# Row sums of one pair of heads taken from ScalarE and given to GpSimd and VectorE, in a fused attention and mixer kernel

## The chip, the core and the metric

The kernel runs on one core of a Trainium2 chip. The metric is the device time of one execution in microseconds, lower being better. PE is TensorE, DVE is VectorE, ACT is ScalarE, POOL is GpSimd, SP is the queue that issues the DMAs.

## What is computed

Four batches of eight heads go through a banded attention, and its result goes through a two-step mixer. Cut to what matters here:

```python
scores_l = scale * q @ k.T                       # kept where |row - column| < 16
scores_s = scale * q @ k_sum.T + log(32)         # k_sum: maxima of 32 keys each
a = exp(scores_all - rowmax(scores_all))
a = a / (sum(a, axis=-1, keepdims=True) + 1e-9)  # the row sums of this change
x = a @ concat([v, v_sum])                       # v_sum: means of 32 values each
h = relu(x.T @ w_tok1) @ w_tok2;  u = x + h.T    # token mixer
out = u + relu(u @ w_ch1) @ w_ch2                # channel mixer
```

## The kernel before

Each batch has four pairs of heads, and each pair's 768 rows are worked off as six tiles of 128 rows, in two groups g of three. For a pair p and a group g, `scores` lets PE make two tiles of products `sc` (one for each head of the pair, 128 x 360). DVE then handles one tile row at a time in `lowest` (L527): it scales, adds the mask, writes the result to `e` and leaves the row's minimum of the negated scores in `den[:, 1]`. ACT follows in `power` (L537): it takes the exponential in place and leaves the row sum in `den[:, 0]`, by its accumulator, which costs a second instruction (ACTIVATION_READ_ACCUMULATOR) behind each exponential. There are 12 exponentials per pair. PE turns `e` around (`et`, L575), ACT copies the turned tile out (`eT`, L586), and PE multiplies it with the values (`av`, L645). POOL adds 1e-9 to the six row sums (`rec`, L651), DVE takes the reciprocal (L671) and scales the product into `x` (L656).

Beside that run, for the first batch: DVE's maxima of the next pair's keys (`ks`, L381) and their copy into the key tile (L390), which the next pair's `sc` needs; the value means, summed by PE (`vm`, L407), copied by ACT (L418), joined by DVE (L428, L421) and POOL (L433); and the unpacking of the mixer's weights, in steps ("ticks") of 512 KB. A tick passes from ACT (L1711) to POOL (L1715), to three steps of DVE (L1720, L1727, L1734), and, for all but the first three, on to ACT (L1758) and POOL (L1764), which split a weight into a high and a low part. The first three ticks make `wt1`, the operand of the first mixer product `t1p` (L799); ticks 3 to 5 make `wt2h` and `wt2l`, those of `up` (L966); later ones, with tiles named `wb_6`, `wb_7`, `wb_8`, ..., make the channel mixer's, of which `hp` (L1027) is the first product. A tick's tile `wb` has two buffers at this place, so tick 8 waits until POOL has read tick 6's.

The order on each engine is not written by hand. Every piece of work is given to `Plan.add` with a rank and a guessed duration; the planner walks through a model of the machine and writes each engine's instructions in the order that comes out. `PLACES` overrides the place of single pieces, which it names by their number in the order of the `add` calls. Each engine then works strictly in its order.

Of the kernel before, what the change touches and what calls it, by code (L numbers as in the profile page):

```python
# [14 lines left out]
AF = mybir.ActivationFunctionType  # L15
ALU = mybir.AluOpType
AX = mybir.AxisListType.X
# [6 lines left out]
P = 128  # L24
# [4 lines left out]
NC = WIN + NB  # L29
NP = H // 2  # L30
VB = NP * NB
TT = S // P
# [39 lines left out]
class Work:  # L72
# [5 lines left out]


PLACES = {  # L80
# [11 lines left out]
}  # L92


# [151 lines left out]
def tile_attention_mixer(  # L246
# [13 lines left out]
    nc = tc.nc  # L260
# [6 lines left out]
    add = plan.add  # L267

    def sbuf(shape, tag, name, bufs, dtype=F32):
        return plan.slot(sb, shape, dtype, tag, name, bufs)  # L270
# [10 lines left out]
        out=means[:, NB - 2 : NB],  # L281
        in_=identf[:WIN, 16 : 16 + QT].rearrange("p (r c) -> p r c", c=32),
        axis=AX, op=ALU.add,
# [203 lines left out]
    def scores(p, g, behind=()):  # L487

        kt, qt = k_t[p], q_t[p]
        tiles = []  # L490
        e = e_t[p, g] = sbuf([P, 2, HS], "e", f"e_{p}_{g}", 3)
        if p >= FAR * NP:

            add(
                "pool", 0.2,
                lambda: nc.gpsimd.memset(
                    e.t.rearrange("p j (t c) -> p (j t) c", c=P)[:, :, NC:], 0.0
                ),
                writes=[(e, "ends")], rank=R_LATER,
            )  # L500
        for j in range(2):
            n = 2 * p + j
            if g == 0:
                den_t[n] = sbuf([P, 2, TT], "den", f"den_{n}", 5)
            tiles.append(att_bank(f"sc_{n}_{g}"))

        def products():
            for i in range(TT // 2):
                for c in range(2):
                    t = 2 * (TT // 2 * g + i) + c  # L510
                    for j in range(2):
                        rows = slice(j * D, (j + 1) * D)
                        nc.tensor.matmul(  # L513
                            tiles[j].t[c * QT : (c + 1) * QT, i * NC : (i + 1) * NC],
                            lhsT=qt.t[rows, t * QT : (t + 1) * QT], rhs=kt.t[rows, t, :],
                            start=True, stop=True,
                        )

        add(
            "pe", 0.95, products, reads=[(qt, 0), (kt, 0), (kt, 1)],  # L520
            writes=[(t, 0) for t in tiles], rank=R_H, behind=behind,
        )

        def lowest(n, j, i):
            T = TT // 2 * g + i
            mv = 0 if T == 0 else (2 if T == TT - 1 else 1)
            nc.vector.tensor_tensor_reduce(  # L527
                out=e.t[:, j, i * P : i * P + NC],
                in0=tiles[j].t[:, i * NC : (i + 1) * NC],
                in1=mask_sb[:, mv, :], op0=ALU.add, op1=ALU.min,  # L530
                scale=-1.0 / 8.0, scalar=3.0e38, accum_out=den_t[n].t[:, 1, T : T + 1],
            )

        def power(n, j, i):
            T = TT // 2 * g + i
            ei = e.t[:, j, i * P : i * P + NC]
            nc.scalar.activation(  # L537
                ei, ei, AF.Exp, bias=den_t[n].t[:, 1, T : T + 1], scale=-1.0,
                accum_out=den_t[n].t[:, 0, T : T + 1],
            )  # L540

        for i in range(TT // 2):
            for j in range(2):
                n = 2 * p + j
                den, T = den_t[n], TT // 2 * g + i
                add(
                    "dve", 0.21, lambda n=n, j=j, i=i: lowest(n, j, i), reads=[(tiles[j], 0), ("mask", 0)],
                    writes=[(e, (j, i)), (den, ("min", T))], rank=R_ATT,
                )
                add(  # L550
                    "act", 0.39, lambda n=n, j=j, i=i: power(n, j, i), reads=[(den, ("min", T))],
                    writes=[(e, (j, i)), (den, ("sum", T))], rank=R_ATT,
                )


    FAR = 2
# [1386 lines left out]
```

## Time and profile before

| | us |
|---|---|
| median of 3 runs | 556.57 (556.07, 556.57, 558.44) |
| the profiled execution | 557.6 |
| its span, from the first to the last instruction | 555.8 |
| PE busy in the span | 543.1 |
| ACT busy, DVE busy, POOL busy | 251.8, 330.6, 246.7 |

The span is what the views of the trace divide up; 1.8 us of the profiled execution's time lie outside it. A busy PE is one with a product under way. [...]

### The profile page before, as it was taken

To read this page: it belongs to the slowest core of one execution; us is meant where nothing else is said; L and a number is where in the kernel's file an instruction comes from. 1 tells how busy PE (TensorE), PEld (TensorE's weight loads), DVE (VectorE), ACT (ScalarE), POOL (GpSimd) and SP (SyncE) were. 2 spreads that over 40 slices of the span, in tenths; PEclk is the share of its full clock that TensorE was granted. 3 is DMA by queue.
4 is the path that set the end of the run, shared out by engine and by line. 5 is a ranking of instruction groups with operands and counts; after the bars stand their busy time and mean duration, and the time that the engine had idled before them with its cause. 6 is when DMAs were issued, how large, how long until landed. Compare 5 with 4: busy or idle time off the path is not lost.

```text
span 555.8 us, 12577 instructions
## 1 busy us (share of the span) xinstructions
PE 543.1 (98%) x4549; PEld 478.7 (86%) x4549; DVE 330.6 (59%) x922; ACT 251.8 (45%) x784; POOL 246.7 (44%) x362
## 2 busy tenths in 40 slices
PE   7799999999999999999999999999999999999997
PEld 4589788889989878888799987878889999999997
DVE  5897799988463355553553257344352066569992
ACT  5895666526485443322414325243433443356410
POOL 0356688726383933310058404467869853000000
PEclk9999999999999999999999999999999999999999
DMA  8992568745658147867676216787696543932732
GB/s 294 343 255 85 184 197 261 245 131 190 228 163 256 38 153 208 224 190 210 160 229 157 96 30 202 164 235 199 168 276 147 135 166 116 317 102 86 238 113 86
DMA packets 125743, 101.10 MB, mean 182 GB/s; under 512 B 70000, under 2 KB 105456, under 8 KB 125680
## 3 DMA queue, kind: packets, MB, share of 16 engines
q1 hardware_dynamic: 125680, 100.29, 60.8%
q8 instruction: 36, 0.59, 0.5%
q14 instruction: 27, 0.22, 0.1%
HBM read 70.18 MB, written 28.31 MB: 177 GB/s over the span
## 4 chain that ended last, share of the span: by engine, by line
PE 88%; DVE 5%; POOL 3%; ACT 2%; issue 1%; POOLq 0%; DVEq 0%; ACTq 0%
PE acc L1070 28%; PE hp L1027 27%; PE sc L513 4%; PE av L645 4%; PE t1q L883 3%; PE up L966 3%; PE x L1297 2%; PE y L1297 2%; PE z L1297 2%; PE pz L1297 2%; PE up L1259 2%; PE pw L1297 1%; PE pv L1297 1%; PE px L1297 1%; PE pr L1297 1%; PE w L1297 1%
## 5 line engine op out<-in xcount | busy, mean ns | idle before, releaser
L1070 PE MATMUL acc<-h,w2h 128*128 128x256 f32 (+1 forms) x576 | 153.9, 339 | 0.0
L1027 PE MATMUL hp<-u,w1h 128*128 128x256 f32 (+1 forms) x576 | 143.9, 339 | 0.3 <-DVE u L1010 0.3
L1070 PEld LDWEIGHTS acc<-h,w2h 128*128 128x128 f32 x576 | 100.5, 188 | 13.9 <-ACT h L1039 1.7
L1027 PEld LDWEIGHTS hp<-u,w1h 128*128 128x128 f32 x576 | 98.0, 189 | 12.9 <-issue 1.1
L1027 PE MATMUL hp<-u,w1l 128*128 128x256 f32 (+1 forms) x288 | 96.9, 336 | 0.0
L1070 PE MATMUL acc<-h,w2l 128*128 128x256 f32 (+1 forms) x288 | 96.4, 335 | 0.0
L537 ACT ACTIVATE e<-e,den 128x120 f32<-128x120 f32 x192 | 73.5, 385 | 48.8 <-DVE den L527 37.9
L1044 DVE SCALAR_TENSOR_TENSOR h<-hp,h 128x512 fp32r<-128x512 f32 (+1 forms) x72 | 39.8, 552 | 83.9 <-ACT h L1039 83.8
L1039 ACT ACTIVATE h<-hp 128x512 fp32r<-128x512 f32 (+1 forms) x72 | 35.1, 487 | 104.2 <-PE hp L1027 104.0
L1027 PEld LDWEIGHTS hp<-u,w1l 128*128 128x128 f32 x288 | 54.4, 189 | 5.8
L1070 PEld LDWEIGHTS acc<-h,w2l 128*128 128x128 f32 x288 | 54.2, 188 | 5.2
L527 DVE CUSTOM_DVE_ANT_0 e<-sc,mask_sb 128x120 f32<-128x120 f32 x192 | 41.8, 277 | 14.9 <-PE sc L513 14.3
L537 ACT ACTIVATION_READ_ACCUMULATOR e<-e,den 128x1 f32 x192 | 36.3, 189 | 0.0
L651 POOL TENSOR_SCALAR rec<-den 128x6 f32<-128x6 f32 x32 | 8.5, 266 | 58.7 <-ACT e L537 57.0
L1110 POOL TENSOR_TENSOR ot<-ot,u 128x512 f32<-128x512 f32 (+1 forms) x24 | 24.4, 1045 | 21.4 <-DVE ot L1102 19.9
L469 DVE TENSOR_REDUCE vs<-vb 96x8 f32<-96x256 f32 (+1 forms) x40 | 18.0, 461 | 21.0 <-DMA vb<-in_vb 20.7
L513 PE MATMUL sc<-k,q 64*64 64x120 f32 x768 | 27.7, 271 | 2.2 <-DVE k L390 1.2
L513 PEld LDWEIGHTS sc<-k,q 64*64 64x64 f32 x768 | 20.3, 132 | 10.8 <-issue 7.9
L645 PEld LDWEIGHTS av<-v,eT 120*64 120x64 f32 x768 | 24.1, 138 | 5.3 <-issue 3.5
L966 PE MATMUL up<-wt2h,t 128*128 128x512 f32 (+1 forms) x96 | 28.4, 353 | 0.1
L645 PE MATMUL av<-v,eT 120*64 120x64 f32 x768 | 26.7, 224 | 1.3 <-DVE den L527 0.8
L381 DVE TENSOR_REDUCE ks<-k 128x24 f32<-128x768 f32 x16 | 15.1, 946 | 19.9 <-DMA k<-in_kw 19.8
(248 smaller groups left out, 1042.5 us busy)
## 6 DMA issues: line engine op xcount, KB each, us to landing
w<-in_w_ch SPq DMA_DIRECT2D x48, 256.0 KB
k<-in_kw SPq DMA_DIRECT2D x16, 720.0 KB
v<-in_vw SPq DMA_DIRECT2D x32, 288.0 KB
q<-in_q SPq DMA_DIRECT2D x16, 384.0 KB
away<-e SPq DMA_DIRECT2D x16, 384.0 KB
eT<-away SPq DMA_DIRECT2D x64, 96.0 KB
w<-in_w_tok SPq DMA_DIRECT2D x12, 256.0 KB
vb<-in_vb SPq DMA_DIRECT2D x32, 96.0 KB
```

The costliest lines, as they stand in the source:

```text
L469: lambda: nc.vector.tensor_reduce(out=s.t[:VB, rows], in_=slot.t[:VB], axis=AX, op=ALU.add),
L513: nc.tensor.matmul(tiles[j].t[c * QT : (c + 1) * QT, i * NC : (i + 1) * NC], lhsT=qt.t[rows, t * QT : (t + 1) * QT], rhs=kt.t[rows, t, :], ...
L527: nc.vector.tensor_tensor_reduce(out=e.t[:, j, i * P : i * P + NC], in0=tiles[j].t[:, i * NC : (i + 1) * NC], in1=mask_sb[:, mv, :], op0=A ...
L537: nc.scalar.activation(ei, ei, AF.Exp, bias=den_t[n].t[:, 1, T : T + 1], scale=-1.0, accum_out=den_t[n].t[:, 0, T : T + 1],)
L645: nc.tensor.matmul(pv[cs, T], lhsT=eT[:NC, T % (TT // 2), cs], rhs=v.t[:NC, 2 * T + c], start=True, stop=True,)
L966: nc.tensor.matmul(pt.t[:, :nt], lhsT=t1.t[:, part, ks], rhs=w.t[:, k, h0 : h0 + nt], start=(far and k == 0 and i == 0), stop=(k == DTOK / ...
L1027: nc.tensor.matmul(pt.t[:, :nt], lhsT=block(w, f, c), rhs=us[c].t[:, part], start=(i == 0), stop=(i == len(ops) - 1),)
L1039: lambda: nc.scalar.activation(h.t[:, 0], pt.t[:, :nt], AF.Relu),
L1044: lambda: nc.vector.scalar_tensor_tensor(out=h.t[:, 1], in0=pt.t[:, :nt], scalar=0.0, in1=h.t[:, 0].bitcast(F32), op0=ALU.max, op1=ALU.sub ...
L1070: nc.tensor.matmul(slot.t[:, c0 : c0 + nt], lhsT=block(w, f, o), rhs=h.t[:, part], start=(f == 0 and w == "w2h" and part == 0 and o % n == 0),
L1110: lambda view=view, u=u: nc.gpsimd.tensor_tensor(out=view(), in0=view(), in1=u.t[:, 1].bitcast(F32), op=ALU.add),
L1297: nc.tensor.matmul(pt.t[:, :cols], lhsT=w[wp][0](), rhs=z.t[:, zp], start=first and seen == 0, stop=final and seen == 3 * len(ops) - 1, sk ...
```

## The change

For the first pair alone (p = 0), the exponentials of ACT no longer use the accumulator. The row sums come from a new function, `totals`, called once for each group: POOL adds three strips of 40 columns of `e` onto each other for all six tile rows (two additions of 128 x 240), folds the 40 columns to 20 (one addition of 128 x 120), and DVE sums the 20 columns, in one reduction for each of the two heads (128 x 3 results). That is 6 additions and 4 reductions for the pair. The tile `some` of the partial sums has one buffer, shared with a tile that the start of the program uses for warming up PE. All other pairs keep the accumulator. Ten more pieces of work stand in the list, so later pieces have other numbers, and `PLACES` holds another set of places altogether; two of its lines stand here for all.

```diff
 PLACES = {
-    6: (0, 3.73), 23: (1, 279.8), 30: (1, 279.88), 34: (1, 88.42), 36: (1, 279.87),
+    4: (0, 3.2), 6: (0, 2.9), 16: (2, 32.7), 35: (2, 13.2), 36: (2, 126.1), 39: (2, 13.7),
...
             ei = e.t[:, j, i * P : i * P + NC]
+            total = den_t[n].t[:, 0, T : T + 1] if p >= 1 else None
             nc.scalar.activation(
-                ei, ei, AF.Exp, bias=den_t[n].t[:, 1, T : T + 1], scale=-1.0,
-                accum_out=den_t[n].t[:, 0, T : T + 1],
+                ei, ei, AF.Exp, bias=den_t[n].t[:, 1, T : T + 1], scale=-1.0, accum_out=total
             )
...
+        if p < 1:
+            totals(p, g)
+
+    def totals(p, g):
+        e, third = e_t[p, g], NC // 3
+        some = sbuf([P, TT, third], "vb", f"some_{p}_{g}", 1)
+        def part(i):
+            return e.t.rearrange("p j (t c) -> p (j t) c", c=P)[:, :, i * third : (i + 1) * third]
+        def more(a, b):
+            nc.gpsimd.tensor_tensor(out=some.t, in0=a(), in1=b(), op=ALU.add)
+        def fold():
+            nc.gpsimd.tensor_tensor(
+                out=some.t[:, :, : third // 2], in0=some.t[:, :, : third // 2],
+                in1=some.t[:, :, third // 2 :], op=ALU.add,
+            )
...
+        for j in range(2):
...
+                lambda j=j, den=den, T=T: nc.vector.tensor_reduce(
+                    out=den.t[:, 0, T : T + TT // 2],
+                    in_=some.t[:, TT // 2 * j : TT // 2 * (j + 1), : third // 2],
+                    axis=AX, op=ALU.add,
+                ),
```

What the change moves was read from the order of the instructions before and after. On all engines the order differs up to about the first ten products of the channel mixer's first sums and is the same from there to the end. In names such as `sc_2_0` the first number is the head, the second the group.

On ACT, the twelve exponentials of the first pair stand group by group (before, the two groups are mixed), and three copies of turned tiles (`eT`) stand among them instead of one. On PE, the turns of the first pair that follow `et_0_0`, namely `et_1_0` and `et_0_1`, come before `sc_2_0`, not after it. On SP, the loads of `q_3` and `k_3` stand ahead of `v_4`, not behind it; `v_7` stands behind the two halves of tick 5; the other loads up to the channel weights keep their places.

DVE, from the key maxima of pair 1 on. Before:

```order
L381 TENSOR_REDUCE ks_1_170<-k_1_99 128x24
L527 ISA e_0_1_156,den_0_141<-sc_0_1_126,mask_sb_71 128x120
L527 ISA den_0_141 128x1
L390 COPY k_1_99<-ks_1_170 128x12x24
L527 ISA e_0_1_156,den_1_143<-sc_1_1_127,mask_sb_71 128x120
L527 ISA den_1_143 128x1
L671 RECIPROCAL rec_0_201<-rec_0_201 128x6
L527 ISA e_1_0_231,den_2_232<-sc_2_0_186,mask_sb_71 128x120
```

After:

```order
L392 COPY k_1_99<-ks_1_180 128x12x24
L529 ISA e_0_1_162,den_1_149<-sc_1_1_127,mask_sb_71 128x120
L529 ISA den_1_149 128x1
L591 TENSOR_REDUCE den_0_141<-some_0_0_177 128x3
L591 TENSOR_REDUCE den_1_149<-some_0_0_177 128x3
L529 ISA e_1_0_228,den_2_229<-sc_2_0_205,mask_sb_71 128x120
...
L591 TENSOR_REDUCE den_0_141<-some_0_1_222 128x3
L591 TENSOR_REDUCE den_1_149<-some_0_1_222 128x3
L430 TENSOR_TENSOR vs_0_0_282<-vm_0_231,vs_0_0_282 24x64
L423 TENSOR_TENSOR v_1_103<-vm_0_231,vs_0_0_282 24x768
L716 RECIPROCAL rec_0_289<-rec_0_289 128x6
```

The reductions stand where DVE has finished a group's scores, so DVE comes to them in its order whether POOL's additions are done or not.

PE, between the products of the third pair and the first mixer product. Before:

```order
L575 MATMUL et_4_0_499<-identf_66,e_2_0_423 120x128 x3
L575 MATMUL et_5_0_520<-identf_66,e_2_0_423 120x128 x3
L575 MATMUL et_4_1_529<-identf_66,e_2_1_495 120x128 x3
L407 MATMUL vm_2_534<-v_4_330,means_72 24x64
...
L575 MATMUL et_5_1_588<-identf_66,e_2_1_495 120x128 x3
L799 MATMUL t1p_0_0_597<-x_0_0_357,wt1_371 128x128 x12
```

After:

```order
L620 MATMUL et_4_0_514<-identf_66,e_2_0_403 120x128 x3
L620 MATMUL et_5_0_533<-identf_66,e_2_0_403 120x128 x3
L409 MATMUL vm_2_542<-v_4_375,means_72 24x64
...
L620 MATMUL et_4_1_596<-identf_66,e_2_1_510 120x128 x3
L620 MATMUL et_5_1_602<-identf_66,e_2_1_510 120x128 x3
L844 MATMUL t1p_0_0_608<-x_0_0_373,wt1_406 128x128 x12
```

One turn, `et_4_1`, has gone behind `vm_2` and `sc_6_0`; otherwise the same work stands ahead of `t1p_0_0`.

DVE, where the last `x` of the batch are made and ticks 6 to 8 pass (`t1p_0_3` on PE needs both). Before:

```order
L785 SCALAR_TENSOR_TENSOR t1_0_2_830<-t1p_0_2_793,t1_0_2_830 128x256
L656 TENSOR_TENSOR x_0_1_694<-av_6_817,rec_6_765 128x6x64
L1720 TENSOR_SCALAR wb_6_815<-wb_6_815 128x512
L656 TENSOR_TENSOR x_0_1_694<-av_7_833,rec_7_772 128x6x64
L1727 SCALAR_TENSOR_TENSOR wb_6_815<-w_6_514,wb_6_815 128x512
L1720 TENSOR_SCALAR wb_7_848<-wb_7_848 128x512
L1734 SCALAR_TENSOR_TENSOR wb_6_815<-w_6_514,wb_6_815 128x512
```

After:

```order
L430 TENSOR_TENSOR vs_0_3_822<-vm_3_786,vs_0_3_822 24x64
L423 TENSOR_TENSOR v_7_519<-vm_3_786,vs_0_3_822 24x768
L1779 SCALAR_TENSOR_TENSOR wb_6_769<-w_6_524,wb_6_769 128x512
L1765 TENSOR_SCALAR wb_7_847<-wb_7_847 128x512
L1772 SCALAR_TENSOR_TENSOR wb_7_847<-w_7_708,wb_7_847 128x512
L1055 TENSOR_TENSOR u_0_0_0_873<-up_0_0_0_831,u_0_0_0_873 128x512
L701 TENSOR_TENSOR x_0_1_675<-av_7_855,rec_7_773 128x6x64
L1779 SCALAR_TENSOR_TENSOR wb_7_847<-w_7_708,wb_7_847 128x512
L1765 TENSOR_SCALAR wb_8_896<-wb_8_896 128x512
L701 TENSOR_TENSOR x_0_1_675<-av_6_902,rec_6_771 128x6x64
```

The `x` of head 6 has gone behind the first DVE step of tick 8 (L1765, before L1720), and tick 6's last DVE step ahead of both `x`.

## Rows read from the trace of the kernel before

**Rows 1.** Busy time of each engine in three stretches of the span: length, then busy us and instructions of PE, of PE's weight loads, of DVE, ACT and POOL, granted clock, DMA share, GB/s.

```profile
8.30:30.00 21.70, 15.30 (x356) 11.59 (x360) 18.70 (x94) 19.95 (x88) 5.39 (x10) 1.00 1.04 325
30.00:61.00 31.00, 30.53 (x404) 27.49 (x392) 26.48 (x72) 22.22 (x69) 19.45 (x26) 1.00 0.55 163
61.00:555.80 494.80, 490.16 (x3744) 436.62 (x3744) 282.94 (x750) 208.13 (x627) 221.11 (x319) 1.00 0.60 175
```

**Rows 2.** Who waited for whom in the first 90 us, PE alone: us in total, times, longest.

```profile
PE et L575 <- DVE x L656: 1.4, 2, 1.1
PE sc L513 <- DVE k L390: 1.2, 1, 1.2
...
PE et L575 <- ACT eT L586: 1.0, 2, 0.6
```

**Rows 3.** Timeline of PE: start, us, then the instructions merged, with the idle time before them and what ended it. The first `sc` is `sc_2_0`, the second `sc_6_0`; the `vm` is `vm_2`; the three `t1p` are `t1p_0_0`, `t1p_0_2` and `t1p_0_3`.

```profile
11.22 1.08 PE L513 MATMUL sc<-k,q 64*64 64x120 f32 x24 [1.18 <-DVE k L390]
...
29.52 0.87 PE L407 MATMUL vm<-v,means 96*24 96x64 f32 x48
30.32 0.84 PE L513 MATMUL sc<-k,q 64*64 64x120 f32 x24
31.09 0.54 PE L575 MATMUL et<-identf,e 128*120 128x128 f32 x3
31.48 2.84 PE L799 MATMUL t1p<-x,wt 128*128 128x128 f32 x24
...
41.86 2.84 PE L799 MATMUL t1p<-x,wt 128*128 128x128 f32 x24
...
51.77 2.84 PE L799 MATMUL t1p<-x,wt 128*128 128x128 f32 x24
...
60.94 0.73 PE L1027 MATMUL hp<-u,w1h 128*128 128x512 f32 x2 [0.32 <-DVE u L1010]
```

**Rows 4.** Timeline of ACT, in the same columns: the first exponential of the program and the next, the turned copy among them, two copies that follow each other, and the last exponential of the first pair.

```profile
8.05 0.39 ACT L537 ACTIVATE e<-e,den 128x120 f32<-128x120 f32 x1 [6.05 <-DVE den L527]
8.35 0.18 ACT L537 ACTIVATION_READ_ACCUMULATOR e<-e,den 128x1 f32 x1
8.44 0.38 ACT L537 ACTIVATE e<-e,den 128x120 f32<-128x120 f32 x1
...
10.71 0.47 ACT L586 ACTIVATE eT<-et 120x384 f32<-120x384 f32 x1
11.08 0.38 ACT L537 ACTIVATE e<-e,den 128x120 f32<-128x120 f32 x1
...
12.97 0.38 ACT L537 ACTIVATE e<-e,den 128x120 f32<-128x120 f32 x1
...
13.46 0.44 ACT L418 ACTIVATE vs<-vm 24x64 f32<-24x64 f32 x2
...
44.66 0.72 ACT L1758 ACTIVATE wt2h<-wb 128x256 fp32r<-128x256 f32 x2 [1.47 <-DVE wb L1734]
```

**Rows 5.** Timeline of DVE: the copy of pair 1's keys, the end of the last scores of the first pair, the first scores of the second, a wait for its other group, the copy of pair 3's keys and the last two steps of `wt1`.

```profile
10.82 0.31 DVE L390 COPY k<-ks 128x288 f32<-128x288 f32 x1
...
11.24 0.08 DVE L527 DVE_READ_ACCUMULATOR2_ANT den<- 128x1 f32 x1
...
12.34 0.28 DVE L527 CUSTOM_DVE_ANT_0 e<-sc,mask_sb 128x120 f32<-128x120 f32 x1 [0.23 <-PE sc L513]
...
18.88 0.28 DVE L527 CUSTOM_DVE_ANT_0 e<-sc,mask_sb 128x120 f32<-128x120 f32 x1 [0.88 <-PE sc L513]
...
29.77 0.30 DVE L390 COPY k<-ks 128x288 f32<-128x288 f32 x1
29.99 0.68 DVE L1727 SCALAR_TENSOR_TENSOR wt<-w,wt 128x512 int32<-128x512 int32 x1
...
30.71 0.69 DVE L1734 SCALAR_TENSOR_TENSOR wt<-w,wt 128x512 int32<-128x512 int32 x1
31.32 0.28 DVE L527 CUSTOM_DVE_ANT_0 e<-sc,mask_sb 128x120 f32<-128x120 f32 x1
```

**Rows 6.** POOL's subtractions of 128 x 256 in its timeline, two by two: the first two beside DVE's L527, the second two beside DVE's weight steps; and, from the page, its additions of 128 x 512 (us of all, then mean ns of one).

```profile
36.78 1.43 POOL L1764 TENSOR_TENSOR wt2l<-wb,wt2h 128x256 fp32r<-128x256 f32 x2
...
50.17 2.52 POOL L1764 TENSOR_TENSOR w1l<-wb,w1h 128x256 fp32r<-128x256 f32 x2 [2.06 <-ACT w1h L1758]
L1110 POOL TENSOR_TENSOR ot<-ot,u 128x512 f32<-128x512 f32 (+1 forms) x24 | 24.4, 1045 | 21.4 <-DVE ot L1102 19.9
```

**Rows 7.** The one DVE reduction of few elements in the program (busy us, mean ns).

```profile
L280 DVE TENSOR_REDUCE means<-identf 96x2 f32<-96x64 f32 x1 | 0.2, 216 | 0.2 <-POOL identf masks.py:199 0.2
```

**Rows 8.** Ticks 6 and 8 in the timelines of DVE, ACT and POOL: the DVE step behind `t1p_0_2` and the `x` after it; tick 6's last DVE step; tick 8's ACT step, POOL step and first DVE step, with the idle time before each.

```profile
46.26 0.43 DVE L785 SCALAR_TENSOR_TENSOR t<-t1p,t 128x256 fp32r<-128x256 f32 x1 [1.64 <-ACT t L780]
46.60 0.55 DVE L656 TENSOR_TENSOR x<-av,rec 128x384 f32<-128x384 f32 x1
...
48.96 0.68 DVE L1734 SCALAR_TENSOR_TENSOR wb<-w,wb 128x512 int32<-128x512 int32 x1
...
52.73 0.76 ACT L1711 ACTIVATE wb<-w 128x256 f32<-128x256 f32 x2 [1.78 <-POOL w1l L1764]
53.65 0.61 POOL L1715 TENSOR_SCALAR wb<-wb 128x512 f32<-128x512 f32 x1 [0.95 <-ACT wb L1711]
54.30 0.95 DVE L1720 TENSOR_SCALAR wb<-wb 128x512 int32<-128x512 int32 x1 [2.19 <-POOL wb L1715]
```

**Rows 9.** Busy share of the DMA engines from 5 to 28.5 us, in 40 slices, in tenths.

```profile
DMA  9999899999999999999999999999999999999999
```

More of the change, by code (lines that the diff above doesn't have):

```diff
@@ L550, in scores @@
                 add(
-                    "act", 0.39, lambda n=n, j=j, i=i: power(n, j, i), reads=[(den, ("min", T))],
-                    writes=[(e, (j, i)), (den, ("sum", T))], rank=R_ATT,
-                )
+                    "act", 0.39 if p >= 1 else 0.22, lambda n=n, j=j, i=i: power(n, j, i),
+                    reads=[(den, ("min", T))],
+                    writes=[(e, (j, i))] + [(den, ("sum", T))] * (p >= 1), rank=R_ATT,
+                )
+        if p < 1:
[12 more added lines that the diff above has]
+            )
+        parts = [(e, (j, i)) for j in range(2) for i in range(TT // 2)]
+        add(
+            "pool", 0.7, lambda: more(lambda: part(0), lambda: part(1)), reads=parts,
+            writes=[(some, 0)], rank=R_ATT,
+        )
+        add(
+            "pool", 0.7, lambda: more(lambda: some.t, lambda: part(2)), reads=parts,
+            writes=[(some, 0)], rank=R_ATT,
+        )
+        add("pool", 0.45, fold, writes=[(some, 0)], rank=R_ATT)
+        for j in range(2):
+            den, T = den_t[2 * p + j], TT // 2 * g
+            add(
+                "dve", 0.14,
+                lambda j=j, den=den, T=T: nc.vector.tensor_reduce(
[3 more added lines that the diff above has]
+                ),
+                reads=[(some, 0)],
+                writes=[(den, ("sum", T + i)) for i in range(TT // 2)], rank=R_ATT,
+            )
     FAR = 2
```

22 rows, old and new, of the table PLACES are left out of this document.

## The prediction

> **What bounds the kernel now.** The first view to read is busy time by stretch [rows 1]. From 61 us to the end PE is busy for 490.2 of 494.8 us, and from 30 to 61 us for 30.5 of 31.0. Only from 8.3 to 30 us, while the first attention batch gets going, does PE have slack: 15.30 of 21.70 us busy, 6.40 us idle. Since the change leaves the order alone behind the channel mixer's first products, all it can give back is these 6.40 us and the 0.47 us of the next stretch. It removes no PE work.
>
> The second view, who waited for whom on PE, says what that slack is [rows 2]: many short waits, mostly for DVE (its `x`, its key copy) and for ACT's turned copies. The third look is at the two engines that feed PE there: ACT is busy for 19.95 of 21.70 us and DVE for 18.70 [rows 1]. So DVE has only 3.00 us of idle time to give up, and DVE is what ends the slack: the key copy of pair 3 is done at 29.99 and `sc_6_0`, which needs it, starts at 30.32; the last step of `wt1` is done at 31.32 and `t1p_0_0` starts at 31.48 [rows 3, 5]. From there on PE has enough to do.
>
> **ACT's part.** Before, an exponential and its read-out step ACT by 0.39 us (8.05 to 8.44), and the last of the first pair's twelve ends at 12.97 + 0.38 = 13.35 [rows 4]. Without the read-out no such exponential is in the trace. Two copies of 64 columns take 0.44 us together and two of 256 columns 0.72, so 120 columns lie between 0.22 and 0.36 each; I take 0.25, nearer the smaller. A turned copy steps ACT by 0.37 (10.71 to 11.08) [rows 4]. Three of them now stand among the twelve: 8.05 + 12 x 0.25 + 3 x 0.37 = 12.16, so the pair is 1.2 us earlier with two more copies behind it. The first group is done at 8.05 + 6 x 0.25 = 9.55.
>
> **POOL's part.** Its additions have no row of their own. The subtractions of 256 columns beside DVE's L527 took 1.43 us for two, 0.715 each; the additions of 512 columns 1.045 on average [rows 6]. That is 1.3 ns a column: 0.695 for 240 columns, 0.54 for 120, so a chain of 0.695 + 0.695 + 0.54 = 1.93 us for each group. The upper bound is the pair that took 2.52 us, 1.26 each [rows 6], which would make a chain 3.4 us; it ran beside DVE's weight steps, of which there are none here yet, so I stay at the lower row. The chains end at 9.6 + 1.93 = 11.55 and 12.2 + 1.93 = 14.15. POOL has 16 us of idle time in this stretch [rows 1], which hides the 3.9 us; the two `rec` and the `v` copy queued behind the chains are due only when DVE has made `v_1`, a us later.
>
> **DVE's part.** Four reductions are added. The bounds are 0.10 each and the 0.216 of the one small reduction [rows 7]; with 20 columns in six rows I take 0.14, 0.56 in all. They also make DVE wait in its own order, with pair 1's scores queued behind the first two and the `v_1` step behind the last two. It comes to the first at about 11.25 (the last read-out of the first pair is at 11.24 [rows 5]) and waits 0.3 us for POOL. `sc_2_0` now stands behind `et_0_1`, whose third exponential is done at 9.55 + 0.37 + 4 x 0.25 = 10.92; with a turn of 0.39 (31.09 to 31.48 [rows 3]) it starts near 11.4, not 11.22. Its scores begin 1.12 us after it, as before (11.22 to 12.34 [rows 3, 5]), near 12.5: a wait of 0.65 after the reductions. Six scores end at 13.75, and the second chain's sums come at 14.15: 0.4 more. Together 1.35, say 1.4 with the handovers. In return the old waits go: the second group of pair 1, for which DVE sat idle 0.88 us until 18.88 [rows 5], is on PE some 4 us sooner (11.4 + 0.77 + a turn of 0.39 + a `vm` of 0.80, then 1.1 to its scores: 14.5), and DVE has work in hand from 14.5 on. The same steps stand ahead of `wt1`'s last one in both orders, so it ends at 31.32 - 3.00 + 1.4 + 0.56 = 30.3, 1.0 us earlier. The key copy of pair 3 now stands behind one more weight step of 0.60: 29.99 - 1.04 + 0.60 = 29.55.
>
> **PE's part.** `sc_6_0` starts at 29.6 rather than 30.32, 0.7 us sooner, but one turn that stood ahead of it now follows (0.39). With 0.77 for `sc_6_0` (30.32 to 31.09) and two turns, `t1p_0_0` starts at 29.6 + 0.77 + 0.78 = 31.15, not 31.48 [rows 3]: **0.3 us gained**. Half a dozen waits in front of it disappear into this one figure, since DVE is last either way.
>
> From there two more places count. `t1p_0_3`, at 51.77 before, could start at 51.45, but the `x` that it needs now stands on DVE behind tick 8's first step, which came at 54.30, released by POOL [rows 8]. Tick 8 is earlier too. Four items that preceded `t1p_0_2` on PE now follow it (a `vm` of 0.80 and three turns, 1.17), so it starts at 41.86 - 0.3 - 2.0 = 39.6 and ends at 42.4 [rows 3]; DVE's step behind it comes near 43.0, not 46.26 with its wait of 1.64; and through one `v` step (0.97), a weight step and a short wait tick 6's last step ends near 46.0, not 49.6 [rows 8]. From that end to tick 8's first step it took 54.30 - 49.64 = 4.7 us, 2.52 of them POOL's two slow subtractions [rows 6, 8]. So tick 8 comes between 49.6 (at 1.43) and 50.7, and with its step (0.95) and the `x` (0.55) [rows 8], which overlap a little, the `x` is there between 51.0 and 52.2. I put **0.3 us** of waiting there. Last, the 0.32 us that PE waited before `hp` [rows 3] should go, as DVE's ticks run some 3 us ahead: **0.3 us gained**.
>
> **The loads.** The DMA engines are busy in every slice from 5 to 28.5 us [rows 9], so SP's new order moves arrivals within one stream: `q_3` and `k_3` sooner by one `v` tile, `v_4` later, `v_5` where it was, and `vm_2` needs both `v`. `v_7`, behind 512 KB more, is wanted two `t1p` later than before (2.84 each [rows 3]). I cost the queue at nothing; without that cover, `vm_2` would wait.
>
> **The sum.** Against the profiled execution: 557.6 - 0.3 + 0.3 - 0.3 = 557.3. That execution lies 1.0 us above the median of the runs, so 556.3. Bounds: with no wait for POOL, reductions of 0.10 and no wait at `t1p_0_3` it is 1.2 less, 555.1; with POOL's chain at its upper bound DVE is 1.5 later, 557.8. The lowest run lies 0.5 under the median, which I add on both sides: 554.6 to 558.3.
>
> **The rivals.** *POOL is slow.* If its additions run at the 1.26 us row, the second sums come 1.5 us later, DVE passes that on, and the gain at `t1p_0_0` turns into a loss: 557.8. For it speaks that DVE waits there twice; against it that the neighbours are L527 steps.
>
> *A copy that POOL holds up.* DVE's key copy of pair 1 at 10.82 [rows 5] falls into the first chain. Were it held until an addition ends, up to 0.7 us, `sc_2_0` would come 0.4 later and the last exponential of the first pair 0.3; then 556.6. The trace before has no POOL work beside that copy, so no row decides. [...]
>
> *The `x` waits for tick 8 (slower).* If DVE or POOL do not bring tick 6 forward, tick 8 stays at 54.30, the `x` is done at 55.7, and PE stands idle from 51.45 on: 4.2 us, less the 0.3 at `hp`, 560.2 in all. It decides once tick 8 is later than about 50.0; half of the full delay makes 558.4. For it speaks that the margin I worked out is about nil; against it that all the work ahead of tick 6 on DVE is counted above.
>
> *The read-outs stay, or cost nothing.* If the exponentials still step by 0.38, the first pair ends at 13.7, 1.5 later than forecast, and so do the second sums: 557.7.
>
> *Everything fits.* DVE's 3.00 us of idle time, less 0.56, and the 0.3 at `hp` are all that can come back: 2.7 us, 553.9. That would need PE's and DVE's waits to vanish at once.
>
> **How the numbers follow.** About 0.5%, 2.8 us here, is what a measurement can tell from no change. Chances: forecast 0.55, slow POOL 0.13, held copy 0.09, read-outs 0.04, `x` behind tick 8 0.13 (0.10 of it beyond 2.8 us), everything fits 0.06 (0.05 of it beyond, were a bound of mine too tight). So faster 0.05, same 0.85, slower 0.10. The range leaves out most of the last two rivals.
>
> **What would show it.** ACT's first pair should be done near 12.2 us with steps near 0.25; POOL's chains should take about 1.9 us each; DVE should wait at both pairs of reductions, 0.3 and 0.4 us; `t1p_0_0` should start near 31.2, and PE should be idle about 6 us from 8.3 to 30 us still, `t1p_0_3` waiting at most 0.8 us. I am wrong if `t1p_0_0` moves by more than a us, if PE waits at `t1p_0_3` for long, or if the stretch behind 61 us differs.

## The result

The changed kernel takes **562.32 us** (median of six runs, 561.57 to 564.4), the kernel before 556.67 (median of six, 556.07 to 558.44): a ratio of **1.0086, 95% interval 1.0059 to 1.0112**. The forecast was 556.3 us and 554.6 to 558.3. It is 0.9% slower, outside the range and on a side that I had given one chance in ten.

The profiled execution took 562.37 us, with a span of 560.6. Lines have moved: DVE's scores from L527 to L529, the key copy from L390 to L392, the exponentials from L537 to L540, the turns from L575 to L620, `av` to L690, `x` from L656 to L701, `t1p` from L799 to L844, `hp` from L1027 to L1072, the weight steps from L1715, L1720, L1727, L1734 to L1760, L1765, L1772, L1779. First, busy time by stretch of the kernel after, in the columns of [rows 1]:

```profile
8.30:30.00 21.70, 18.14 (x312) 13.24 (x312) 17.56 (x79) 16.20 (x62) 8.24 (x15) 0.76 0.94 301
30.00:61.00 31.00, 27.63 (x391) 24.73 (x392) 27.37 (x81) 21.92 (x74) 16.47 (x23) 0.94 0.51 151
61.00:560.60 499.60, 496.04 (x3787) 442.15 (x3786) 287.94 (x758) 212.17 (x635) 224.48 (x324) 1.00 0.60 175
```

Up to 30 us PE is busier than before (18.14 of 21.70 us against 15.30), yet it has done fewer products (312 against 356): the granted clock (TensorE's, as a share of its full speed) is 0.76 there, not 1.00. ACT is relieved (16.20 against 19.95), though the twelve read-outs are only a part of the 26 instructions that it has fewer there, and POOL has 2.85 us more. PE is idle for 3.56 us there, where the forecast had about 6. Then PE's timeline, in the columns of [rows 3]:

```profile
6.26 1.46 PE L515 MATMUL sc<-k,q 64*64 64x120 f32 x48 [0.77 <-DVE k L392]
8.34 1.69 PE L620 MATMUL et<-identf,e 128*120 128x128 f32 x6 [0.63 <-ACT e L540]
10.37 1.32 PE L620 MATMUL et<-identf,e 128*120 128x128 f32 x3 [0.33 <-ACT e L540]
11.62 1.48 PE L515 MATMUL sc<-k,q 64*64 64x120 f32 x24
...
20.06 1.32 PE L690 MATMUL av<-v,eT 120*64 120x64 f32 x24
21.31 0.85 PE L515 MATMUL sc<-k,q 64*64 64x120 f32 x24
...
32.92 0.54 PE L620 MATMUL et<-identf,e 128*120 128x128 f32 x3 [2.00 <-DVE x L701]
33.39 0.87 PE L409 MATMUL vm<-v,means 96*24 96x64 f32 x48
34.20 1.11 PE L515 MATMUL sc<-k,q 64*64 64x120 f32 x24
35.24 1.53 PE L620 MATMUL et<-identf,e 128*120 128x128 f32 x6
36.57 3.55 PE L844 MATMUL t1p<-x,wt 128*128 128x128 f32 x24
...
67.21 0.63 PE L1072 MATMUL hp<-u,w1h 128*128 128x512 f32 x2
```

`sc_2_0` starts 0.2 us behind its forecast (11.62 against 11.4), but its 24 products take 1.48 us at a granted clock of 0.50 where the 24 of `sc_4_0`, at 21.31, take 0.85 at 1.00. `t1p_0_0` starts at 36.57, not at 31.48 as before nor at the 31.15 of the forecast, and `hp` at 67.21 rather than 60.94 [rows 3]. So 5.1 us are lost ahead of `t1p_0_0` and 1.2 from there to `hp`. Of these 6.3 us, 1.5 are given back behind `hp` in this pair of traces: from `hp` to the end of the span it is 493.4 us against 494.9. That stretch lies between 493.1 and 496.0 in all twenty traces of this study, old order and new alike, so the loss is to be looked for ahead of `hp`.

DVE (rows as in [rows 5]):

```profile
10.60 0.77 DVE L392 COPY k<-ks 128x288 f32<-128x288 f32 x1
...
11.75 0.34 DVE L591 TENSOR_REDUCE den<-some 128x3 f32<-128x60 f32 x2 [0.18 <-POOL some L572]
13.15 0.28 DVE L529 CUSTOM_DVE_ANT_0 e<-sc,mask_sb 128x120 f32<-128x120 f32 x1 [1.06 <-PE sc L515]
...
14.64 0.34 DVE L591 TENSOR_REDUCE den<-some 128x3 f32<-128x60 f32 x2 [0.19 <-POOL some L572]
15.89 0.22 DVE L430 TENSOR_TENSOR vs<-vm,vs 24x64 f32<-24x64 f32 x1 [0.91 <-ACT vs L420]
...
21.43 0.56 DVE L701 TENSOR_TENSOR x<-av,rec 128x384 f32<-128x384 f32 x1 [1.50 <-PE av L690]
...
24.91 1.00 DVE L1765 TENSOR_SCALAR wt<-wt 128x512 int32<-128x512 int32 x1
...
33.84 0.31 DVE L392 COPY k<-ks 128x288 f32<-128x288 f32 x1
34.06 0.68 DVE L1779 SCALAR_TENSOR_TENSOR wt<-w,wt 128x512 int32<-128x512 int32 x1
```

The sums' own waits are small (0.18 and 0.19). The three that count, 1.06, 0.91 and 1.50 us, are for products of PE, or for what ACT makes of them, and all three begin while the granted clock is 0.50 (below). The steps on `wt1` start at 24.91, not 21.50. ACT's first six exponentials and the last of the pair, POOL's chain, and the clock where it fell (columns of [rows 1]; the granted clock is the third number from the end):

```profile
7.83 1.82 ACT L540 ACTIVATE e<-e,den 128x120 f32<-128x120 f32 x6 [5.83 <-DVE den L529]
...
12.11 0.39 ACT L540 ACTIVATE e<-e,den 128x120 f32<-128x120 f32 x1
```

```profile
9.73 0.69 POOL L569 TENSOR_TENSOR some<-e 128x240 f32<-128x240 f32 x1 [8.42 <-ACT e L540]
10.51 0.70 POOL L569 TENSOR_TENSOR some<-some,e 128x240 f32<-128x240 f32 x1
11.28 0.44 POOL L572 TENSOR_TENSOR some<-some 128x120 f32<-128x120 f32 x1
```

```profile
10.00:11.00 1.00, 0.67 (x3) 0.27 (x2) 1.00 (x4) 1.00 (x5) 0.92 (x2) 0.87 1.04 273
11.00:12.00 1.00, 0.85 (x10) 0.56 (x13) 0.82 (x5) 1.00 (x4) 0.64 (x2) 0.50 1.03 270
12.00:20.00 8.00, 7.60 (x171) 6.16 (x163) 5.65 (x33) 5.89 (x27) 3.12 (x6) 0.50 1.04 376
...
21.00:22.00 1.00, 1.00 (x36) 0.86 (x32) 0.56 (x1) 0.70 (x3) 0.00 (x0) 1.00 1.04 430
...
35.00:38.00 3.00, 3.00 (x21) 2.76 (x14) 2.69 (x17) 2.34 (x9) 1.59 (x3) 0.50 0.91 245
```

From about 10.7 to 21 us and again from about 34.6 to 38, behind the 2.00 us in which PE stood idle at `et_5_0`, the granted clock is 0.50.

### The profile page after: what moved, and what is told of

It reads as the page before. It is cut to its first block, busy times and chain, and to the rows that moved or that the text cites. A ratio compares the mean times of both kernels' runs of the same rounds, so it can differ in the third digit from the quotient of the medians.

```text
span 560.6 us, 12578 instructions
## 1 busy us (share of the span) xinstructions
PE 547.6 (98%) x4549; PEld 482.9 (86%) x4549; DVE 335.6 (60%) x926; ACT 252.0 (45%) x772; POOL 249.9 (45%) x368
## 4 chain that ended last, share of the span: by engine, by line
PE 92%; DVE 2%; DMA 2%; POOL 1%; ACT 1%; issue 1%; SPq 0%; DVEq 0%; POOLq 0%
PE acc L1115 27%; PE hp L1072 27%; PE av L690 4%; PE up L1011 4%; PE sc L515 4%; PE t1q L928 3%; PE x L1342 2%; PE y L1342 2%; PE z L1342 2%; PE pz L1342 2%; PE et L620 2%; PE t1q L891 2%; PE up L1304 1%; PE t1p L844 1%; PE pw L1342 1%; PE pv L1342 1%
## 5 line engine op out<-in xcount | busy, mean ns | idle before, releaser
L1072 PE MATMUL hp<-u,w1h 128*128 128x256 f32 (+1 forms) x576 | 143.8, 339 | 0.0
L1072 PEld LDWEIGHTS hp<-u,w1h 128*128 128x128 f32 x576 | 98.0, 189 | 12.4 <-issue 1.1
L1072 PE MATMUL hp<-u,w1l 128*128 128x256 f32 (+1 forms) x288 | 96.9, 336 | 0.0
L540 ACT ACTIVATE e<-e,den 128x120 f32<-128x120 f32 x192 | 72.7, 385 | 51.2 <-DVE den L529 42.8
L1072 PEld LDWEIGHTS hp<-u,w1l 128*128 128x128 f32 x288 | 54.4, 189 | 5.8
L529 DVE CUSTOM_DVE_ANT_0 e<-sc,mask_sb 128x120 f32<-128x120 f32 x192 | 42.0, 277 | 15.5 <-PE sc L515 13.6
L540 ACT ACTIVATION_READ_ACCUMULATOR e<-e,den 128x1 f32 x180 | 33.9, 188 | 0.0
L690 PEld LDWEIGHTS av<-v,eT 120*64 120x64 f32 x768 | 25.2, 142 | 6.0 <-issue 3.9
L690 PE MATMUL av<-v,eT 120*64 120x64 f32 x768 | 28.1, 229 | 1.4 <-DVE v L423 1.3
L701 DVE TENSOR_TENSOR x<-av,rec 128x384 f32<-128x384 f32 x32 | 17.3, 552 | 13.7 <-PE av L690 12.8
```

What stands on the lines that cost most here:

```text
L529: nc.vector.tensor_tensor_reduce(out=e.t[:, j, i * P : i * P + NC], in0=tiles[j].t[:, i * NC : (i + 1) * NC], in1=mask_sb[:, mv, :], op0=A ...
L540: nc.scalar.activation(ei, ei, AF.Exp, bias=den_t[n].t[:, 1, T : T + 1], scale=-1.0, accum_out=total)
L690: nc.tensor.matmul(pv[cs, T], lhsT=eT[:NC, T % (TT // 2), cs], rhs=v.t[:NC, 2 * T + c], start=True, stop=True,)
L701: nc.vector.tensor_tensor(out=x2.t[:, :, hp % 2, j * D : (j + 1) * D], in0=pt.t[:, : TT * D].rearrange("p (t d) -> p t d", d=D), in1=rec.t ...
L1072: nc.tensor.matmul(pt.t[:, :nt], lhsT=block(w, f, c), rhs=us[c].t[:, part], start=(i == 0), stop=(i == len(ops) - 1),)
```

## The experiments

Theory 1: the clock makes the loss. Theory 2: the new order does, clock or not. Theory 3: the sums do. Theories 4 and 5 stand with the runs that try them. Ratios are to the kernel before, which ran beside each group of runs (medians 557.7 to 558.4), with 95% intervals.

### Sums or order

**e1_before** is the old kernel unchanged.

> The kernel before, unchanged, to see TensorE's granted clock in several of its runs. Theory 1 (the clock: the 5.6 us are lost because TensorE runs at half clock from 10.8 to 21.0 us and from 34.8 to 38 us) expects 556 to 558 us and a granted clock of 1.000 from the warm-up's end in every run. If runs of before show falls like those of after (a mean of 0.988 to 0.994) at an unchanged time, theory 1 loses most of its ground. Theory 2 (the new order makes VectorE and TensorE wait) and theory 3 (the new sums themselves hold VectorE) expect 556 to 558 us and say nothing of the clock.

558.40 us, 1.0004 (0.9987 to 1.0022). Its trace shows a fall of its own, at a span of 556.0 us:

```profile
8.00:10.00 2.00, 0.94 (x5) 0.40 (x3) 1.81 (x19) 1.98 (x11) 0.00 (x0) 1.00 1.06 301
10.00:12.00 2.00, 0.55 (x15) 0.51 (x18) 1.57 (x6) 1.97 (x11) 0.24 (x1) 1.00 1.03 247
12.00:13.00 1.00, 1.00 (x57) 0.84 (x53) 0.61 (x6) 1.00 (x7) 0.00 (x0) 1.00 1.14 265
13.00:15.00 2.00, 2.00 (x34) 1.47 (x23) 1.91 (x13) 1.60 (x8) 0.82 (x2) 0.51 0.98 314
```

From 8 to 12 us PE was busy for 1.49 of 4 us, and from 13 us the granted clock is 0.51. So the old kernel's clock falls too, and the trace of before, with 1.00 in all three stretches [rows 1], was the exception: of 108 runs of it (twelve of them e1_before's) nine had a mean granted clock of 1.000 (mean time 557.1 us), 34 one of 0.997 (557.5) and 42 one of 0.994 (558.5). From 1.000 to 0.994 its mean time rises by 1.4 us. Theory 1 loses its premise that falls are new; what is new is their length, since after's six runs have 0.988 to 0.994.

**e3_order** is the new order without the sums, by a list of the works' numbers (a work is one piece given to `Plan.add`) in place of the planner:

```diff
-PLACES = {...}
+ORDERED = [2, 0, 3, 1, 6, 4, 5, ...]
     def _order(self):
+        return [self.works[i] for i in ORDERED]
```

> The order of the changed kernel without its sums: its list of works word for word, less the ten works of the sums, with ScalarE's accumulators back. Theory 1: 560 to 562 us if the granted clock falls as in after, 556 to 558 us if it stays at 1.000. Theory 2 (the order): 560 to 562 us, whatever the clock does. Theory 3 (the sums): 556 to 558 us.

562.51 us, **1.0083** (1.0055 to 1.0110): the whole loss, without one POOL addition.

**e2_sums** and **e2b_sums** are the other half: the sums in the old order. They differ in where DVE makes the reductions and the reciprocals of pair 0 (numbers of DVE's works alone, shortened; 106 is the first `x`, 134 the means of `v_3`):

```diff
-e2_sums:  ... 134, 117, 125, [29, 30, 49, 50, 105, 109], 106, ...
+e2b_sums: ... [29, 30, 49, 50], 134, [105, 109], 117, 125, 106, ...
```

> The sums of the changed kernel in before's order: the list of works that before's planner wrote is kept as it stands, with the POOL additions set behind the last exponential of their group and the reductions, 1e-9 additions and reciprocals of pair 0 set just ahead of the first x of pair 0; the second group's sums have a buffer of their own. Theory 1: 556 to 558 us if the granted clock stays at 1.000, 559 to 562 us if it falls. Theory 2 (the order): 556 to 558 us, whatever the clock does. Theory 3 (the sums): 559 to 562 us, whatever the clock does.

559.84 us, 1.0041 (1.0024 to 1.0059); the first `x` came at 20.78 us, 1.5 later than before, behind reductions and reciprocals.

> The sums of the changed kernel in the old order, as in e2_sums, but the four reductions stand on VectorE ahead of v_3's means and the two reciprocals behind them, where VectorE idled 0.88 us in before; in e2_sums all of it stood just ahead of the first x and put that 1.4 us later. Theory 3 (POOL's and VectorE's sums cost by themselves what e2_sums lost): 559 to 561 us. That their place cost it: 557.5 to 558.5 us, the time of before within 0.2%.

558.72 us, **1.0009** (0.9996 to 1.0023). Well placed, the sums cost nothing that can be told from zero, and gain nothing. Theory 3 falls. What their place did is seen in the times alone: in the trace of e2b_sums the first `x` comes at 20.81, no earlier than in e2_sums (with waits of 0.76 and 1.04 us for keys still on their way from memory), so the late `x` does not explain the difference. The runs of e2_sums also had the lower clock: nine of twelve had 0.993 or less, against one of twelve.

Together with the kernel before and the changed one, e3_order and e2b_sums fill a table of two by two: old order 0 and, with the sums, 0.09%; new order 0.83% and, with the sums, 0.86%. The order makes the loss, with the sums or without.

### Which part of the order

**h1_newold18**, **h2_newold30** and **h3_oldnew20** splice the two lists, without sums. Each edit is a long list of numbers; it follows this rule, where `first` is the new order in h1 and h2 and the old one in h3, and `start` is the planner's own time:

```diff
+ORDERED = [w for w in first if w.start < T] + [w for w in rest if it is not in yet]
```

> No sums (ScalarE's accumulators as before). The new order up to the point at which its list has sc_4_0 next (its first 18 us or so), then the old list's order for all that is left. Theory 2a (the new order loses its time in those first works, before sc_4_0) expects 561 to 563 us. Theory 2b (it loses it between sc_4_0 and the first token product, where VectorE has the weight steps of wt1 ahead of the scores of sc_4_1 and of x) and theory 2c (it loses it behind the first token product) expect 557 to 559 us. The old order is at 557.7 us, the new order without the sums at 562.5.

> No sums. The new order up to the first token product t1p_0_0, then the old list's order for all that is left. Theories 2a and 2b: 561 to 563 us. Theory 2c: 557 to 559 us.

> No sums. The old order up to sc_4_0, then the new list's order for all that is left. Theory 2a: 557 to 559 us. Theories 2b and 2c: 561 to 563 us.

562.48 us, 1.0075 (1.0052 to 1.0098); 563.24, 1.0093 (1.0074 to 1.0113); 561.30, 1.0064 (1.0046 to 1.0082). h2_newold30, with the new order only up to `t1p_0_0`, loses as much as the whole. Neither half is innocent, and the losses of the halves do not add up to that of the whole. A splice brings waits of its own, though: in h1 PE stands 2.43 us at a turn for an `x` that the other list has later.

**m1_scores** sets DVE's scores of `sc_4_1`, two `x` (196 and 200) and pair 3's key reduction and copy (154, 155) ahead of steps of `wt1` that preceded them (numbers of works on DVE: 210 to 220 are the scores, 89 to 91 and 96 to 98 the steps):

```diff
-89, 90, 91, 196, 96, 97, 210, 212, 220, 214, 218, 200, 154, 216, 155, 98
+89, 196, 210, 212, 220, 214, 218, 216, 200, 154, 155, 90, 91, 96, 97, 98
```

> The changed kernel with its sums and its order, but on VectorE the six scores of sc_4_1 and the x of av_2 and av_3 stand ahead of the last two steps of wt1's second tile and of its third tile, and so does pair 3's key reduction with its copy. Theory 2b: the 2.0 us that et_5_0 waits for x go, t1p_0_0 starts 1.5 us earlier or more, 559.5 to 561 us. Theory 2a (VectorE has the same work to do and is late when it comes to it): et_5_0 starts earlier, but wt1's last step ends at about 35 us as before, t1p_0_0 does not start before 36 us, and the time stays at 562 to 563 us.

561.83 us, 1.0063 (1.0041 to 1.0086). `et_5_0` starts 2.2 us earlier (30.73) and `t1p_0_0` 3.1 (33.49), but then it waits 0.50 us for `wt1`, later PE waits 0.93 and 1.40 for DVE, and `hp` is only 1.0 us earlier. The wait went elsewhere.

**n1_clamps** (561.51 us, 1.0055, 1.0036 to 1.0074) asks whether POOL's steps make DVE's longer (theory 4):

```diff
-            add("pool", 0.65, lambda: clamp(nc.gpsimd), writes=parts, rank=rank)
+            add("pool", 0.65, lambda: None, writes=parts, rank=rank)
```

> The changed kernel without POOL's clamp of wt1's three tiles (that part is left out and not done elsewhere), everything else in its order. Theory 4 (part of the loss is that VectorE's weight steps run beside POOL's instructions and take longer for it): the steps that took 0.89 and 0.84 us take 0.69 and 0.42, wt1's last step ends at 34.0 us or earlier in place of 34.74, and the time falls by 0.6 to 1.2 us, to 561 to 561.7. Theories 1 and 2: the steps take what they took, or the time stays at 562 to 563 us.

The two steps took 0.68 and 0.42 us, as expected; the one beside POOL's `v` copy, which stayed, took 1.00 still. `wt1`'s last step ended at 33.13, in a trace in which the clock fell less (0.997 in the mean). Against after the time falls by 0.8 us by the medians and by 0.31% by the ratios, with intervals that overlap, and further down the same edit moves nothing (c2_tail against c3_tail).

**d1_after** and **d0_before** leave out three DVE steps:

```diff
-        add("dve", 0.69, shift, reads=parts, writes=[bkey], rank=rank)
+        add("dve", 0.69, (lambda: None) if i == 0 else shift, reads=parts, writes=[bkey], rank=rank)
```

(and `sign` and `low` likewise).

> The changed kernel without VectorE's three steps on wt1's first tile (that part is left out; they took 1.00, 0.89 and 0.69 us in the trace of after). Theory 5 (VectorE's queue): t1p_0_0 starts 1.5 to 2.6 us earlier, the time falls by 1.5 to 2.6 us to 559.7 to 560.8. Theory 1 (TensorE at half clock sets the start of t1p_0_0, VectorE has room): 561.8 to 562.6 us.

> The kernel before without the same three steps (0.43, 0.69 and 0.67 us in the trace of before). If VectorE's queue sets the time in the old order too: 556 to 557 us (1 to 1.8 us less than before). If the old order has room on VectorE: within 0.5 us of before.

562.36 us, 1.0087 (1.0063 to 1.0112), and 559.26, 1.0035 (1.0014 to 1.0055). In the new order 2.6 us of DVE's work less bring nothing; DVE stands 1.06 us waiting for POOL where the steps were, and in this trace PE took 1.47 us for 22 products of `sc_4_1` and 1.55 for the 24 of the `av` behind them (at 28.77 and 30.17), where in after it took 0.84 and 0.92, at a granted clock of 1.00. Theory 5, that VectorE's queue alone sets the time, falls. That the old order became slower with less to do was no theory's expectation, and I have no cause for it; its trace, with a span of 554.9 us, does not show it. Its clock was lower as well (0.994 or less in nine of ten runs, against 48 of the old kernel's 108), but the runs at 0.994 alone took 559.8 us on average, against 558.5.

### The clock

**e4_fill** and **f2_fill** give PE something to do in its gaps: products of the identity with itself (fillers), whose result nobody reads. Both also have 16 warm-up products rather than 13. From e4_fill:

```diff
+                fill(pt, {(0, 0, 0): 3, (0, 1, 0): 2, (2, 0, 0): 3, (2, 0, 1): 9}.get((p, g, j), 0))
```

> The changed kernel with more work for TensorE in its gaps: 16 warm-up products in place of 13, and products of the identity with itself (into the bank that the work then overwrites) ahead of et_0_0 (3), et_0_1 (2), sc_2_0 (2), et_4_0 (3) and et_5_0 (9). Theory 1 expects a granted clock of 1.000 behind the warm-up and with it 556 to 558 us. Theories 2 and 3 expect 561 to 563 us with a granted clock of 1.000. If the clock falls none the less, the run tells nothing on the time.

> The changed kernel with more fillers than e4_fill: 16 warm-up products, and identity products ahead of et_0_0 (4), et_0_1 (3), et_1_1 (2), sc_2_0 (3), av_1 (6), et_2_1 (3), et_3_0 (3), et_3_1 (5), sc_4_1 (2), et_4_0 (4) and et_5_0 (10). To get a trace of the new order with TensorE at full clock. Theory 1 (the clock): at 1.000 the time is 556 to 558 us. Theory 2 (the order, through VectorE): at 1.000 it is 561 to 563 us still, and t1p_0_0 does not start before 34 us.

562.58 us, 1.0079 (1.0064 to 1.0094), and 562.45, 1.0075 (1.0053 to 1.0096), with one and two runs at a granted clock of 1.000 (561.77; 561.15 and 561.55). Both say less about the clock than they seem to: the fillers wrote to the bank of the work that they stood ahead of and waited for it as well, as e4_fill's PE timeline shows, where they start only when `x` has freed the bank:

```profile
32.22 1.21 PE L491 MATMUL et<-identf 128*128 128x128 f32 x9 [0.54 <-DVE x L709]
33.27 0.49 PE L628 MATMUL et<-identf,e 128*120 128x128 f32 x3
```

**f3_fill** writes them to the warm-up's bank, which nobody wants yet, with 13 warm-up products again:

```diff
+                pw.t[:, :P], lhsT=identf, rhs=identf, start=True, stop=True, is_transpose=True
```

> The changed kernel in its own order with fillers that cost nothing of their own: identity products into the warm-up's bank, which is free until the first token product, ahead of et_0_0 (3), et_0_1 (1), et_1_1 (1), av_1 (3), et_2_1 (3), et_3_0 (2), et_3_1 (4), et_4_0 (2) and et_5_0 (8), sized to the waits that stand there in the trace of after. Theory 1 (the clock): the runs that keep a granted clock of 0.997 or more are at 556 to 558.5 us. Theory 5 (VectorE's queue ahead of wt1 sets the start of t1p_0_0): they are at 560 to 562 us still, and wt1's last step does not end before 33.5 us.

560.83 us, 1.0059 (1.0036 to 1.0082); the runs at 0.997 or more took 559.72, 559.94 and 561.23. Theory 1 is worth 1.5 us by the medians, and its interval overlaps that of after. The mean of the three runs at 0.997 or more is 560.3 us; the 44 runs of the kernel before at such a clock have 557.4, so 2.9 us are lost without a low clock (the fillers' own cost included). What the clock hides is seen in busy time from 8.3 us to `hp`, for before, after, f3_fill, and f3_fill's fillers alone (columns of [rows 1]; in the last only PE, its loads and DVE):

```profile
8.30:60.94 52.64, 45.78 (x744) 39.01 (x744) 45.11 (x164) 42.17 (x156) 24.85 (x36) 1.00 0.75 230
```

```profile
8.30:67.21 58.91, 51.98 (x745) 43.37 (x745) 50.73 (x168) 42.57 (x146) 29.86 (x44) 0.88 0.68 210
```

```profile
8.30:65.89 57.59, 52.27 (x768) 43.38 (x769) 50.23 (x172) 42.71 (x147) 30.36 (x44) 0.94 0.74 218
...
8.30:65.89 57.59, 4.59 (x24) 3.01 (x24) 0.00 (x0) 0.94 0.74 218
```

In after, PE is idle for 6.93 us (58.91 - 51.98), as long as in before (6.86), and busy for 6.2 us more: the loss looks like the clock's. In f3_fill the kernel's own products keep PE busy for 47.68 us (52.27 - 4.59), 1.9 more than before, and for 9.91 us it has none to do, 3.05 more. Fillers could themselves hold a product up; m1_scores (the changed kernel but for the move on DVE) has none, and its trace can be laid beside that of e1_before at the same clock, e1_before first:

```profile
8.30:62.02 53.72, 47.14 (x745) 40.20 (x745) 45.30 (x164) 42.37 (x156) 24.82 (x36) 0.97 0.77 225
```

```profile
8.30:66.19 57.89, 48.88 (x749) 40.29 (x745) 50.85 (x174) 42.84 (x147) 30.87 (x44) 0.97 0.71 218
```

PE is busy for 1.7 us more there, and idle for 9.01 us against 6.58. At that clock (0.97, against 0.88 in after) the products of the new order wait longer instead: by the idle times in PE's timeline 3.5 us for ACT and 4.7 for DVE, against 1.1 and 4.3 in e1_before.

### Together

**all3** and **c1_three** are m1_scores, n1_clamps and fillers at once, of f2_fill and of f3_fill.

> Three edits at once in the changed kernel: the fillers of f2_fill, VectorE's order of m1_scores (scores and x ahead of wt1's last steps), and wt1's clamps left out as in n1_clamps. If the clock, the place of the scores and POOL beside VectorE make up the loss: 557 to 559 us. If the new order loses something else besides: 560 to 562 us.

> As all3 (scores and x ahead of wt1's last steps on VectorE, wt1's clamps left out), but with the fillers of f3_fill, which cost nothing of their own. If the clock, the place of the scores and POOL beside VectorE make up the loss: 557.5 to 559.5 us. If the new order loses something else besides: 560.5 to 562 us, as all3.

561.85 us, 1.0066 (1.0046 to 1.0086), and 560.43, 1.0052 (1.0034 to 1.0069). **c2_tail** and **c3_tail** put the old order behind `t1p_0_0`; c3_tail has the clamps back, so that it computes everything.

> c1_three (costless fillers, scores ahead of wt1's last steps, wt1's clamps left out) up to the first token product, and the old list's order from there on. If the new order behind t1p_0_0 is the rest of the loss (theory 2c): 29.5 us from t1p_0_0 to the first hp in place of 32.0, no wait of av_7, and 557.5 to 558.7 us in all, the time of before. If it is not: 560 us or more, as c1_three (560.43).

> As c2_tail with wt1's clamps back in their place on POOL, so that nothing is left out. Theory 2c: 0.5 to 1 us above c2_tail, 558.2 to 559.5 us; otherwise 560.5 us or more.

559.95 us, 1.0034 (1.0016 to 1.0053), and 560.04, **1.0033** (1.0017 to 1.0050). c3_tail lies below after with intervals that do not touch, and above before. Both times fall between what the two theories expected. From `t1p_0_0` to `hp` it is 31.0 us, against 32.0 in c1_three and 29.5 in before, so the old tail does not run as it did; `hp` starts at 64.44:

```profile
33.41 1.06 PE L900 MATMUL t1p<-x,wt 128*128 128x128 f32 x8
34.64 1.60 PE L900 MATMUL t1p<-x,wt 128*128 128x128 f32 x12 [0.17 <-DVE wt L1835]
```

## Why the prediction was wrong

**Where it failed.** The step is DVE's: "The same steps stand ahead of `wt1`'s last one in both orders, so it ends at 31.32 - 3.00 + 1.4 + 0.56 = 30.3." It ended at 34.74 (34.06 + 0.68 above). I took the old waits of 3.00 us as gone and put 1.4 in their place: DVE was idle for 4.18 us from 8.3 us to that end, among them 0.91 and 1.50 us of a kind that I had ruled out with "DVE has work in hand from 14.5 on". And I let every step last as before: DVE's busy time rose by 2.17 us, not 0.56. The reductions were 0.68 of it; the rest is the key copy (0.77 us against 0.31) and steps of `wt1` beside POOL's (1.00 us where 0.43 stood). Before and after, from 8.3 us to the end of that step (columns of [rows 1]; DVE is the third pair):

```profile
8.30:31.40 23.10, 16.70 (x396) 12.73 (x397) 20.09 (x97) 21.29 (x93) 6.00 (x11) 1.00 1.04 320
```

```profile
8.30:34.74 26.44, 20.50 (x386) 15.10 (x390) 22.26 (x97) 19.26 (x76) 8.48 (x16) 0.80 0.94 296
```

PE's part hangs on it: `sc_6_0` at 34.20, not 29.6, and `t1p_0_0` at 36.57, not 31.15. The clock is the second thing that failed: the sum had no term for it and took every product's time from rows at a granted clock of 1.00. From `sc_6_0` to `t1p_0_0` it put 1.55 us, and it was 2.37, at a granted clock of 0.59.

**What stood in its place.** The cause is the order (e3_order 1.0083, e2b_sums 1.0009), which I had followed at three places and taken as unchanged in effect between them. How it loses is shown only in part. Up to `hp`, PE at a granted clock of 0.50 and waits on DVE's chain lie side by side, and taking one away seems to expose the other: by the ratios n1_clamps, f3_fill and m1_scores bring 0.31, 0.27 and 0.23% and d1_after nothing, none of it clear of the noise. That fits two limits side by side; it does not prove them. Fillers, the place of the scores and the old tail together bring 0.5% back (c3_tail). The last 0.33% is not assigned. c3_tail keeps the new order only ahead of `t1p_0_0`; besides that it keeps the sums, worth 0.23% at most by e2b_sums, and its fillers.

**The terms.** ACT: the first six exponentials took 1.82 us, 0.30 each rather than 0.25, and the pair ended at 12.50 rather than 12.16. POOL: additions of 0.69, 0.70 and 0.44, a chain of 1.99 us against 1.93. Reductions 0.17 against 0.14; the 0.10 that I gave as their lower bound stands in no run. Waits for POOL 0.18 and 0.19 against 0.3 and 0.4; the one before `sc_2_0`'s scores 1.06 against 0.65. PE stood idle ahead of `t1p_0_3` for 0.12 us, where I had put 0.3, and the 0.32 us ahead of `hp` went, as forecast. A wait of 0.87 us for `v` ahead of the `av` at 52.91 was not in the sum. The loads cost nothing, as put: in after no wait that the timelines of PE, DVE, ACT and POOL show between 8 and 67 us ends with a load.

**The rivals.** Slow POOL, read-outs that stay, and everything fits did not happen. The `x` did stand behind tick 8, whose first step came at 57.86 us (`x` at 58.20), but PE had products of `up` until 58.69, so it cost at most the 0.12 us above. The held copy did happen: 0.77 us in after, with POOL's addition at 10.51 beside it, against 0.31 at 19.62 and at 33.84, where POOL was idle. It was not the loss: e3_order, without POOL's additions, is as slow, and there the same copy took 0.30.

**Range and chances.** All bounds were of the sums. The noise I added was half a us, from three runs; 108 runs of the old kernel reach from 555.7 to 561.2.

## What to carry to other kernels

Where a change comes with a new order, the order is part of the change, and here it was nearly all of it: follow every wait of the two engines that end the slack through the whole stretch, not the places where the diff is interesting, and credit no old wait as gone until its successor in the new order is known. Where two limits run side by side, undoing one proves little; try the order without the new work and the new work in the old order first. A filler that is to keep TensorE busy must wait for nothing that the next work waits for: those of e4_fill stood 0.54 us for `x` themselves.

## What the runs showed of the hardware

The mean granted clock of the kernel before was under 1.000 in 99 of 108 runs, although its first profile showed 1.000, so one profile at 1.000 does not tell what the next run will do. No long idle time of PE stood ahead of the first fall in after: it came at 10.7 us, and the longest since the warm-up had been 0.77 us, with 0.63 and 0.33 behind it. The warm-up differs from run to run as well: the same 13 products took 5.73 us in before, 5.45 in e1_before, which is the same kernel, and 4.32 in after, where the single product's time falls from 0.63 to 0.38 us. The column of the granted clock does not show this: it reads 1.00 from 1 to 6 us in after. So its 1.00 tells nothing of a product's time during the warm-up.

VectorE's `wt` step of 128 x 512 in L1765 took 0.42 us alone (in after, at 30.24) and 1.00 us beside POOL's copy (24.91), 0.84 beside its clamp (27.57); without the clamp (n1_clamps, at 26.38) 0.42.
